# The start of a fused attention and MoE kernel: the decays' polynomial moved from VectorE to GpSimd, weight loads and three conversions moved ahead, half of the decay stores on ScalarE's queue

## The chip, the cores and the metric

The kernel runs on one core of one Trainium2 chip, in one launch. The metric is the device time in microseconds (us), lower is better. A core has TensorE (PE, matmuls), VectorE (DVE), ScalarE (ACT), GpSimd (POOL) and SyncE (SP), which here only issues DMA transfers. Each engine works through its own list of instructions in order and waits at an instruction until what it needs is there.

## The reference

Attention with forget gates on 32 heads (4 x 8) of 576 positions and width 64, then two feed-forward blocks on the 2304 tokens:

```
scores = scale * q @ k.T
log_f  = log(clip(f, 1e-4, 1));  cum = cumsum(log_f)
scores = where(causal, -1e9, scores + cum[i] - cum[j])
x = softmax(scores) @ v                       # heads side by side: 2304 x 512
h = x @ w_in;  x = (h * tanh(softplus(h))) @ w_out
x = (((x @ w1) * (x @ w2)) @ w3) @ w_out2
```

The weights arrive as 64-bit floats (looked at as pairs of 32-bit words), and the kernel turns them into 32-bit numbers itself.

## The kernel before

**Phase A** (to about 350 us) is the attention, 16 pairs of heads, each in four slots (0 to 3): scores into PSUM, softmax, transposes, product with v. Between the pieces of attention PE does filler: first eight units `wp_unit`, which multiply w3 by w_out2, 24 matmuls each, then the first layer's matmuls. **Phase B** is the feed-forward. PE's list is written by hand in both phases. The start, up to the end of the first ten weight pieces, is written by hand for ACT, DVE and SP as well; later work of those engines is placed by a scheduler with priorities and `behind` constraints.

**The start** has two strands. The first is the *decays*: `decay_log` (L249) loads f and computes its logarithm on DVE as exponent plus a polynomial of s, with z = s*s: nine instructions to z, then the polynomial (L264 to L267, nine instructions on 128x144), then e, the exponent's part (L268), and the sum (L269). `decay_rows` (L272) sums it along the positions (L279), adds offsets by a matmul with `heads` (L280, L282), splits it into four rows of high and low parts (`slot`, last written at L288), stores them to DRAM by four SP transfers (L290) and loads them back by `load_cum` (L336) as rows of `aug`. PE's first full scores are the sum of q*k from `raw` and the decays from `aug`, so they wait for the whole strand.

The second strand is the *weight pieces* `first`: t00, o0 to o3, t01, o4 to o7, where t is w3 and o is w_out2, 512 KB each. Each is loaded by SP (`cv_load`, L122), gets its exponents and mantissas by ACT (`cv_exp`, L133) and three DVE instructions (`cv_bits`, L141 to L143), and is then split into a high part by ACT (L98) and a low part by DVE (L102). The first `wp_unit` needs all ten. `go(i)` is the exp and the bits of piece i, `fin(i)` the split. The first softmax is held behind piece number HOLD. The next weight pieces (t10, t11 and on) go the same way, but their low parts are taken by POOL (L112).

POOL's part at the start is `consts` (identity, `heads`, the masks m1 and m4) and in `zeros` (L311) the constant fill of `raw`, `aug`, `pt4` and `vb` for both buffers.

What the change touches stands in this order before (the tenth line converts piece 0 while the matmul of the offsets runs):

```python
        self.consts()
        with self.tc.manual_schedule(engines=...Activation, DVE, SP):
            self.zeros()
            self.decay_log()
            self.load_raw(0)
            early(0, NEAR)
            self.decay_rows(lambda: go(0), lambda: early(NEAR, NEAR + 1))
            early(NEAR + 1, len(first))
            for i in range(1, len(first)):
                go(i); ...; fin(i - 1)
            fin(9)
```

Of the kernel before, what the change touches and what calls it, by code (L numbers as in the profile page):

```python
# [33 lines left out]
KQ = 2 * S + 64  # L34
LAST = 2 * S - 64
HOLD = 4
# [7 lines left out]
NEAR = 4  # L44
# [31 lines left out]
class Kernel:  # L76
# [172 lines left out]
    def decay_log(self):  # L249
# [5 lines left out]
        nc.sync.dma_start(x, self.f)  # L255
        dve.tensor_scalar(x, x, 1e-4, 1.0, ALU.max, ALU.min)
# [7 lines left out]
        dve.tensor_scalar(q, z, 1.0 / 17, None, ALU.mult)  # L264
        for k in (15, 13, 11, 9, 7, 5, 3):
            dve.scalar_tensor_tensor(q, q, 1.0 / k, z, ALU.add, ALU.mult)
        dve.scalar_tensor_tensor(q, q, 1.0, s, ALU.add, ALU.mult)  # L267
        dve.tensor_scalar(e, e, 126.0, 0.6931471805599453, ALU.subtract, ALU.mult)  # L268
        dve.scalar_tensor_tensor(q, q, 2.0, e, ALU.mult, ALU.add)  # L269
        self.lf = q  # L270

    def decay_rows(self, between, after):  # L272
# [6 lines left out]
        dve.tensor_tensor_scan(cum, self.lf, self.lf, 0.0, ALU.add, ALU.bypass)  # L279
# [9 lines left out]
        for i in range(4):  # L289
            nc.sync.dma_start(self.cum_scr[:, :, 144 * i:144 * i + 144], f32(slot[32 * i:32 * i + 32]))  # L290
# [4 lines left out]
    def consts(self):  # L295
# [3 lines left out]
        for i in range(1, 4):  # L299
            nc.gpsimd.affine_select(self.heads, self.heads, [[-1, 128]], ALU.not_equal, 1.0, base=32 * i,  # L300
                                    channel_multiplier=1)
        nc.gpsimd.memset(self.m1, 0.0)
# [8 lines left out]
    def zeros(self):  # L311

        nc = self.nc
        for i in range(2):
            nc.vector.memset(f32(self.aug[i]), 0.0)
            for r in (0, 64):
                nc.gpsimd.memset(f32(self.aug[i][r:r + 4, 0:S]), 1.0)
                nc.gpsimd.memset(f32(self.aug[i][r:r + 4, S:LAST if r else 2 * S]), 1.0)
            nc.gpsimd.memset(f32(self.aug[i][64:68, 2 * S:KQ]), 1.0)
            nc.gpsimd.memset(self.raw[i][0:64, 2 * S:2 * S + 64], 0.0)  # L320
            nc.gpsimd.memset(self.raw[i][64:128, LAST:2 * S], 0.0)
            nc.gpsimd.memset(self.pt4[i][64:128], 0.0)
            nc.gpsimd.memset(self.vb[i][64:128], 0.0)
# [277 lines left out]
    def phase_a(self):  # L601
# [23 lines left out]
        self.consts()  # L625
        self.lo_eng = "dve"
        with self.tc.manual_schedule(engines={getattr(mybir.EngineType, e) for e in ("Activation", "DVE", "SP")}):
# [708 lines left out]
```

## Time and profile before

| | us |
|---|---|
| median of 3 runs | 924.03 (923.31 to 926.38) |
| the profiled execution, its own time | 920.79 |
| its span, first to last instruction | 919.0 |
| PE busy | 873.7 (95%) |
| DVE busy | 688.1 (75%) |
| ACT busy | 483.3 (53%) |
| POOL busy | 166.2 (18%) |

The busy shares are averages over the whole span. The rows further down show the first 60 us, where the change is made. Times in them are from the start of the span; a row that begins with two numbers gives the start and the time of an instruction or of a merged run of equal ones ("x4").

### The profile page before, as it was taken

The numbers are of one execution on the slowest core, as the hardware profiler recorded it, in microseconds if no ns is written. First come the engines' busy times: TensorE is split into PE (matmuls) and PEld (weight loads), VectorE is DVE, ScalarE is ACT, GpSimd is POOL, SyncE is SP. The second block draws the span as 40 slices with busy tenths as digits, with TensorE's granted clock in tenths as the row PEclk, the third lists the DMA queues.
The fourth block names the chain that finished last, engine by engine and source line by source line (L and its number), as shares of the span: only waits on it lengthen the run. The fifth ranks groups of instructions, "written<-read, shape, count | busy, mean of one in ns | idle before, by whom it ended". The sixth has DMA issues, their size and how long they took to land.

```text
span 919.0 us, 17491 instructions
## 1 busy us (share of the span) xinstructions
PE 873.7 (95%) x6338; PEld 806.1 (88%) x6338; DVE 688.1 (75%) x1361; ACT 483.3 (53%) x1035; POOL 166.2 (18%) x253
## 2 busy tenths in 40 slices
PE   2799999999999989799999999999999999999998
PEld 1577778888888758799999999999999999999998
DVE  8987796744767676788888889888788887544483
ACT  3766667655556454655645455455784545322152
POOL 4043333325778740000000000000000000000000
PEclk9899999999999999999999999999999999999999
DMA  6965567757788872244475549988986555555552
GB/s 186 273 193 171 174 195 223 214 159 231 247 274 277 286 239 89 70 138 138 138 229 161 184 165 337 368 316 296 413 303 190 153 168 169 161 164 166 174 166 78
DMA packets 129191, 190.12 MB, mean 207 GB/s; under 512 B 12352, under 2 KB 70736, under 8 KB 129104
## 3 DMA queue, kind: packets, MB, share of 16 engines
q1 hardware_dynamic: 114608, 172.66, 58.2%
q10 hardware_dynamic: 14496, 16.33, 5.8%
q8 instruction: 50, 0.82, 0.4%
q14 instruction: 37, 0.30, 0.1%
HBM read 131.44 MB, written 57.52 MB: 206 GB/s over the span
## 4 chain that ended last, share of the span: by engine, by line
PE 63%; DMA 7%; DVE 7%; POOL 5%; issue 2%; ACT 1%; SPq 0%; ACTq 0%; DVEq 0%; POOLq 0%
PE ps_x L993 15%; PE ps_x L1065 14%; PE ps_z L1065 7%; PE ps_l L552 6%; PE ps_z L993 6%; PE ps_y L993 6%; PE ps_y L1065 3%; DMA ws<-ws 2%; PE ps_s L371 2%; PE ps_s L472 2%; POOL pt L849 2%; DMA ws<-pt 1%; PE ps_t L438 1%; POOL pt L848 1%; DVE TX L955 1%
## 5 line engine op out<-in xcount | busy, mean ns | idle before, releaser
L552 PE MATMUL ps_l<-x,wi 128*128 128x288 f32 x696 | 103.2, 302 | 0.6 <-ACT h L556 0.6
L552 PEld LDWEIGHTS ps_l<-x,wi 128*128 128x128 f32 x696 | 94.8, 190 | 5.7 <-issue 2.8
L954 ACT CAST g_h<-y 128x576 fp32r<-128x576 f32 x96 | 63.6, 675 | 55.0 <-PE ps_x L993 26.1
L993 PE MATMUL ps_x<-g_h,ws 128*128 128x288 f32 x512 | 91.5, 297 | 0.9 <-ACT g_h L954 0.7
L955 DVE TENSOR_TENSOR g_l<-y,g_h 128x576 fp32r<-128x576 f32 x96 | 72.3, 753 | 16.1 <-ACT g_h L954 15.3
L401 ACT ACTIVATE P<-P,sum 128x256 f32<-128x256 f32 (+3 forms) x112 | 70.5, 631 | 24.7 <-DVE sum L391 14.6
L993 PEld LDWEIGHTS ps_x<-g_h,ws 128*128 128x128 f32 x512 | 75.8, 189 | 1.8 <-ACT g_h L954 1.2
L391 DVE CUSTOM_DVE_ANT_0 P<-ps_s,m 128x256 f32<-128x256 f32 (+2 forms) x96 | 48.4, 553 | 18.9 <-PE ps_s L371 18.9
L993 PE MATMUL ps_x<-g_l,ws 128*128 128x288 f32 x256 | 55.2, 297 | 0.5 <-DVE g_l L955 0.5
L453 DVE COPY pt<-ps_t 128x128 f32<-128x128 f32 (+1 forms) x64 | 29.7, 485 | 34.5 <-PE ps_t L438 33.8
L1065 PE MATMUL ps_x<-T,gs 128*128 128x288 f32 x384 | 53.8, 295 | 0.9 <-ACT Cg L1070 0.9
L371 PE MATMUL ps_s<-raw 64*128 64x128 f32 (+3 forms) x256 | 46.6, 476 | 8.3 <-DMA raw<-in_qk_dram 5.9
L1065 PE MATMUL ps_x<-T,ws 128*128 128x288 f32 x384 | 53.8, 295 | 0.0
L1065 PEld LDWEIGHTS ps_x<-T,gs 128*128 128x128 f32 x384 | 51.8, 188 | 1.1 <-ACT Cg L1070 1.1
L1065 PEld LDWEIGHTS ps_x<-T,ws 128*128 128x128 f32 x384 | 51.9, 188 | 0.0
L521 PE MATMUL ps_l<-wo,w3h 128*128 128x512 f32 x128 | 45.3, 423 | 5.2 <-DVE wo L102 4.0
L954 ACT CAST h_h<-ab 128x576 fp32r<-128x576 f32 x48 | 31.7, 673 | 34.0 <-PE ps_x L993 19.9
L993 PE MATMUL ps_x<-h_h,ws 128*128 128x288 f32 x256 | 46.3, 297 | 1.5 <-DMA ws<-ws 1.4
L955 DVE TENSOR_TENSOR h_l<-ab,h_h 128x576 fp32r<-128x576 f32 x48 | 35.9, 754 | 15.6 <-ACT h_h L954 15.5
L472 PE MATMUL ps_s<-pt,va 128*64 128x320 f32 (+3 forms) x384 | 45.0, 383 | 0.0
L438 PE MATMUL ps_t<-ident,P 128*128 128x128 f32 x288 | 40.2, 275 | 2.5 <-ACT pt L453 2.2
L993 PEld LDWEIGHTS ps_x<-g_l,ws 128*128 128x128 f32 x256 | 41.2, 189 | 1.0 <-DVE g_l L955 1.0
(278 smaller groups left out, 2180.0 us busy)
## 6 DMA issues: line engine op xcount, KB each, us to landing
ws<-ws SPq DMA_DIRECT2D x112, 512.0 KB
ws<-gs SPq DMA_DIRECT2D x84, 256.0 KB
ws<-pt SPq DMA_DIRECT2D x45, 256.0 KB
h_scr<-h ACTq DMA_DIRECT2D x64, 144.0 KB
y<-h_scr SPq DMA_DIRECT2D x16, 576.0 KB
cvrt<-in_w3t_dram SPq DMA_DIRECT2D x16, 512.0 KB
cvri<-in_w_in_dram SPq DMA_DIRECT2D x16, 512.0 KB
cvru<-in_w_out_dram SPq DMA_DIRECT2D x16, 512.0 KB
```

The lines of the kernel that those rows point to most:

```text
L371: mm(ps[:, 512 * hh:512 * hh + n], t[r, q0:q0 + 128], t[r, 0:n], start=first, stop=not first)
L391: dve = ttr(P[hh][:, :n], ps[:, 512 * hh:512 * hh + n], self.m1[:, 512 - n:], -0.125, 3.0e38, ALU.add, ALU.min, st[hh])
L401: ins = nc.scalar.activation(t[:, :n], t[:, :n], AF.Exp, bias=b, scale=-1.0, accum_out=self.sums[:, i:i + 1])
L438: tr(self.ps_t[hh][:, o + 128 * k:o + 128 * k + 128], P[:, 128 * k:128 * k + 128], self.ident)
L453: return copy(dst[:, 0:c + 1, 128 * c:128 * c + 128], src)
L472: mm(ps[64 * hh:64 * hh + 64, 256 + q:256 + q + w], lhs, rhs, start=i == 0, stop=i == len(plan) - 1)
L521: mm(o, w, x, start=i == 0, stop=i == 23)
L552: mm(o[:, :TB], w, x, start=i == 0, stop=i == 11)
L954: self.mark(self.nc.scalar.copy(hi, raw))
L955: self.mark(self.nc.vector.tensor_tensor(lo, raw, f32(hi), ALU.subtract))
L993: mm(ps[:, r, :TB], w[:, 256 * a + 128 * e:256 * a + 128 * e + 128], ops[i][b][:, r], start=o in (1, 5, 2) and f == 0 and (a, b) == (0, 0) ...
L1065: mm(bank[:, r, :TB], w[:, i:i + 128], T[o, k][:, b, r], start=o in (1, 2, 5) and (k, a, b) == (0, 0, 0), stop=(k, a, b) == (1, 1, 0), ski ...
```

## The change

The polynomial leaves DVE and becomes sixteen POOL instructions, eight with one input and eight with two, each of which reads the result of the one before. DVE keeps e and the sum, which moves to the head of `decay_rows`. SP loads t00 and o0 ahead of `raw`, and o1, o2, o3 and t01 behind it, before the decay stores (six pieces in place of four). Three pieces (t00, o0, o1) are converted, and two of them split, before `decay_rows`, and o1's split stands where t00's conversion stood. Two of the four decay stores are issued by ACT. POOL's fills are put in order by hand: what the first pair needs, the polynomial, then masks and the second buffers. HOLD is 6, and the slots whose loads stand behind the start's are 0 to 7 (before: 0 and 1).

```diff
-HOLD = 4
+HOLD = 6
...
-NEAR = 4
+NEAR = 6
...
-    def decay_log(self):
+    def decay_log(self, after):
...
         nc.sync.dma_start(x, self.f)
+        after()
...
         dve.tensor_tensor(z, s, s, ALU.mult)
-        dve.tensor_scalar(q, z, 1.0 / 17, None, ALU.mult)
-        for k in (15, 13, 11, 9, 7, 5, 3):
-            dve.scalar_tensor_tensor(q, q, 1.0 / k, z, ALU.add, ALU.mult)
-        dve.scalar_tensor_tensor(q, q, 1.0, s, ALU.add, ALU.mult)
         dve.tensor_scalar(e, e, 126.0, 0.6931471805599453, ALU.subtract, ALU.mult)
-        dve.scalar_tensor_tensor(q, q, 2.0, e, ALU.mult, ALU.add)
-        self.lf = q
+        pool = nc.gpsimd
+        pool.tensor_scalar(q, z, 1.0 / 17, 1.0 / 15, ALU.mult, ALU.add)
+        for k in (13, 11, 9, 7, 5, 3, 1):
+            pool.tensor_tensor(q, q, z, ALU.mult)
+            pool.tensor_scalar(q, q, 1.0 / k, None, ALU.add)
+        pool.tensor_tensor(q, q, s, ALU.mult)
+        self.lf = q, e
...
-        dve.tensor_tensor_scan(cum, self.lf, self.lf, 0.0, ALU.add, ALU.bypass)
+        lf, e = self.lf
+        dve.scalar_tensor_tensor(lf, lf, 2.0, e, ALU.mult, ALU.add)
+        dve.tensor_tensor_scan(cum, lf, lf, 0.0, ALU.add, ALU.bypass)
...
-            nc.sync.dma_start(self.cum_scr[:, :, 144 * i:144 * i + 144], f32(slot[32 * i:32 * i + 32]))
+            (nc.sync, nc.scalar)[i % 2].dma_start(self.cum_scr[:, :, 144 * i:144 * i + 144], f32(slot[32 * i:32 * i + 32]))
...
-        def go(i):
-            self.cv_exp(first[i][0])
-            self.last = self.cv_bits(first[i][0])
...
+        def exp(i):
+            if i < len(first):
+                self.cv_exp(first[i][0])
+
+        def bits(i):
+            exp(i + 1)
+            last = self.cv_bits(first[i][0])
+            if i == HOLD:
+                self.hold = last
...
+            self.consts()
             self.zeros()
-            self.decay_log()
+            self.blanks(0)
+            self.ones(0)
+            self.decay_log(lambda: early(0, 2))
             self.load_raw(0)
-            early(0, NEAR)
-            self.decay_rows(lambda: go(0), lambda: early(NEAR, NEAR + 1))
+            early(2, NEAR)
+            self.masks()
+            self.blanks(1)
+            self.ones(1)
+            exp(0)
+            for i in range(3):
+                bits(i)
+                if i:
+                    fin(i - 1)
+            self.decay_rows(lambda: fin(2), lambda: early(NEAR, NEAR + 1))
             early(NEAR + 1, len(first))
-            for i in range(1, len(first)):
-                go(i)
-                if i == HOLD:
-                    self.hold = self.last
-                fin(i - 1)
+            for i in range(3, len(first)):
+                bits(i)
+                if i > 3:
+                    fin(i - 1)
             fin(9)
...
-                with self.behind(self.go_sp if s < 2 else None):
+                with self.behind(self.go_sp if s < 8 else None):
```

PE's list has the same 2155 rows in the same order. The lists of the other engines differ at the start, as shown next, and here and there by one place near the end of phase B.

DVE's list at the decays, before: `lg` holds the logarithm's temporaries, `cvt` and `cvo` are pieces, `cu` the decays' rows.

```order
L263 TENSOR_TENSOR lg_152<-lg_151 128x144
L264 TENSOR_SCALAR lg_152<-lg_152 128x144
L266 SCALAR_TENSOR_TENSOR lg_152<-lg_152 128x144 x7
L267 SCALAR_TENSOR_TENSOR lg_152<-lg_152,lg_151 128x144
L268 TENSOR_SCALAR lg_151<-lg_151 128x144
L269 SCALAR_TENSOR_TENSOR lg_152<-lg_152,lg_151 128x144
L279 SCALAR_TENSOR_TENSOR cu_185<-lg_152 128x144
L141 TENSOR_SCALAR cvt_189<-cvt_189 128x512
L142 SCALAR_TENSOR_TENSOR cvt_189<-cvrt_177,cvt_189 128x512
L143 SCALAR_TENSOR_TENSOR cvt_189<-cvrt_177,cvt_189 128x512
L282 COPY cu_185<-ps_l_82 128x1
```

The same place of the change, from the last piece that is converted ahead of the decays (the conversions of t00 and o0 and t00's low part stand just before these rows, behind z and e):

```order
L141 TENSOR_SCALAR cvo_202<-cvo_202 128x512
L142 SCALAR_TENSOR_TENSOR cvo_202<-cvro_167,cvo_202 128x512
L143 SCALAR_TENSOR_TENSOR cvo_202<-cvro_167,cvo_202 128x512
L102 TENSOR_TENSOR wo_0_216<-cvo_197,wo_0_216 128x512
L282 SCALAR_TENSOR_TENSOR lg_132<-lg_132,lg_131 128x144
L283 SCALAR_TENSOR_TENSOR cu_219<-lg_132 128x144
L102 TENSOR_TENSOR wo_1_224<-cvo_202,wo_1_224 128x512
L286 COPY cu_219<-ps_l_82 128x1
```

The nine polynomial rows are gone, the scan (L279, now L283) stands behind three conversions, and only one low part stands between it and the copy of the offsets.

POOL's list of the change, from the last fill of the first pair's `aug` on; the eleven alternating rows left out are of the same two kinds:

```order
L328 MEMSET aug_95 4x512
L329 MEMSET aug_95 4x64
L267 TENSOR_SCALAR lg_132<-lg_132 128x144
L269 TENSOR_TENSOR lg_132<-lg_132 128x144
L270 TENSOR_SCALAR lg_132<-lg_132 128x144
...
L271 TENSOR_TENSOR lg_132<-lg_132,lg_131 128x144
L309 MEMSET m_86 128x512
L310 MEMSET m_87 128x288
L311 AFFINE_SELECT m_86<-m_86 128x128
```

Before, these sixteen rows did not exist and POOL had no arithmetic until the low part of t10.

DVE's list a little later, where t10 and t11 are converted, the pieces that PE needs for its second `wp_unit` (before, t10 is cvt_337 and t11 cvt_384; `P` rows are softmax):

```order
L141 TENSOR_SCALAR cvt_337<-cvt_337 128x512
L397 ISA P_0_103,sum_307<-ps_s_79,m_86 128x288
L397 ISA sum_307 128x1
L142 SCALAR_TENSOR_TENSOR cvt_337<-cvrt_321,cvt_337 128x512
L398 ISA P_0_103,sum_307<-ps_s_79,m_87,sum_307 128x288
L398 ISA sum_307 128x1
L141 TENSOR_SCALAR cvt_384<-cvt_384 128x512
L143 SCALAR_TENSOR_TENSOR cvt_337<-cvrt_321,cvt_337 128x512
```

And with the change (t10 is cvt_344, t11 cvt_391):

```order
L411 ISA P_0_103,sum_314<-ps_s_79,m_86 128x288
L411 ISA sum_314 128x1
L102 TENSOR_TENSOR wo_7_300<-cvo_286,wo_7_300 128x512
L412 ISA P_0_103,sum_314<-ps_s_79,m_87,sum_314 128x288
L412 ISA sum_314 128x1
L141 TENSOR_SCALAR cvt_344<-cvt_344 128x512
L141 TENSOR_SCALAR cvt_391<-cvt_391 128x512
L142 SCALAR_TENSOR_TENSOR cvt_344<-cvrt_328,cvt_344 128x512
L142 SCALAR_TENSOR_TENSOR cvt_391<-cvrt_330,cvt_391 128x512
L143 SCALAR_TENSOR_TENSOR cvt_344<-cvrt_328,cvt_344 128x512
```

t10 is finished one row later in relation to what surrounds it: t11's second instruction (L142) now stands ahead of t10's last.

## Rows read from the trace of the kernel before

**Rows 1.** PE's waits in the first 48 us: total, times, longest.

```profile
PE ps_s L371 <- DMA aug<-cum_scr: 9.5, 1, 9.5
...
PE ps_l L521 <- DVE wo L102: 4.0, 2, 2.3
```

**Rows 2.** Windows: stretch, busy us of PE to POOL, granted clock, DMA share, GB/s.

```profile
34.00:36.00 2.00, 0.70 (x2) 0.60 (x3) 2.00 (x6) 1.41 (x5) 0.00 (x0) 0.67 1.09 240
...
40.00:42.00 2.00, 2.00 (x8) 1.59 (x6) 1.76 (x6) 1.67 (x4) 0.00 (x0) 0.62 0.97 247
...
50.00:60.00 10.00, 10.00 (x54) 7.32 (x52) 8.36 (x26) 7.99 (x25) 1.44 (x2) 1.00 0.46 149
```

**Rows 3.** PE's timeline: first full scores, last transposes before t10, t10's first matmuls.

```profile
20.75 1.38 PE L371 MATMUL ps_s<-aug 64*128 64x128 f32 x4 [9.46 <-DMA aug<-cum_scr]
...
42.10 0.84 PE L438 MATMUL ps_t<-ident,P 128*128 128x128 f32 x6
44.11 0.74 PE L521 MATMUL ps_l<-wo,w3h 128*128 128x512 f32 x2 [1.17 <-ACT w3h L98]
```

**Rows 4.** DVE's timeline, the decays from behind z to the last slot row.

```profile
6.13 0.23 DVE L264 TENSOR_SCALAR lg<-lg 128x144 f32<-128x144 f32 x1
...
9.07 0.67 DVE L268 TENSOR_SCALAR lg<-lg 128x144 f32<-128x144 f32 x1
9.78 0.31 DVE L269 SCALAR_TENSOR_TENSOR lg<-lg,lg 128x144 f32<-128x144 f32 x1
10.12 0.46 DVE L279 TENSOR_TENSOR_SCAN cu<-lg 128x144 f32<-128x144 f32 x1
...
12.40 0.15 DVE L282 COPY cu<-ps_l 128x1 f32<-128x1 f32 x1
...
13.53 0.23 DVE L288 TENSOR_SCALAR cu<-cu 128x144 fp32r<-128x144 f32 x1
```

**Rows 5.** PE's timeline: the matmul of the offsets.

```profile
10.73 0.56 PE L280 MATMUL ps_l<-cu,heads 128*128 128x1 f32 x2 [2.44 <-DVE cu L279]
```

**Rows 6.** SP's timeline: the four decay stores.

```profile
13.85 2.58 SPq L290 DMA_DIRECT2D cum_scr<-cu x4
```

**Rows 7.** DVE's timeline: start of one piece's bits, the low part behind, the next bits.

```profile
16.49 0.42 DVE L141 TENSOR_SCALAR cvo<-cvo 128x512 int32<-128x512 int32 x1
...
18.27 0.68 DVE L102 TENSOR_TENSOR wo<-cvo,wo 128x512 fp32r<-128x512 f32 x1
18.87 0.42 DVE L141 TENSOR_SCALAR cvo<-cvo 128x512 int32<-128x512 int32 x1
```

**Rows 8.** DVE's timeline: an idle, t10's last instruction, one of t11 beside POOL.

```profile
14.09 0.43 DVE L141 TENSOR_SCALAR cvo<-cvo 128x512 int32<-128x512 int32 x1 [0.33 <-ACT cvo L133]
...
42.43 0.68 DVE L143 SCALAR_TENSOR_TENSOR cvt<-cvrt,cvt 128x512 int32<-128x512 int32 x1
...
44.56 1.11 DVE L143 SCALAR_TENSOR_TENSOR cvt<-cvrt,cvt 128x512 int32<-128x512 int32 x1
```

**Rows 9.** POOL's timeline: a fill, arithmetic beside busy and idle DVE, a dependent pair.

```profile
5.19 0.57 POOL L317 MEMSET aug<- 4x576 f32 x1
...
44.21 4.35 POOL L112 TENSOR_TENSOR w3l<-cvt,w3h 128x256 fp32r<-128x256 f32 x4 [33.09 <-ACT w3h L98]
54.26 1.44 POOL L112 TENSOR_TENSOR w3l<-cvt,w3h 128x256 fp32r<-128x256 f32 x2 [5.70 <-ACT w3h L98]
...
68.35 1.57 POOL L112 TENSOR_TENSOR x<-xx,x 128x288 fp32r<-128x288 f32 x2 [2.32 <-ACT x L98]
...
302.90 0.40 POOL L848 CAST pt<-cvu 128x256 fp32r<-128x256 f32 x1
...
304.12 0.85 POOL L848 CAST pt<-cvu 128x256 fp32r<-128x256 f32 x1
...
306.77 0.72 POOL L829 TENSOR_TENSOR pt<-cvu,cvu 128x256 f32<-128x256 f32 x1
307.57 0.73 POOL L830 TENSOR_TENSOR pt<-pt,cvu 128x256 f32<-128x256 f32 x1
```

More of the change, by code (lines that the diff above doesn't have):

```diff
@@ L301, in consts, with masks @@
                                     channel_multiplier=1)
+    def masks(self):
+        nc = self.nc
         nc.gpsimd.memset(self.m1, 0.0)
@@ L311, in zeros, with ones, blanks @@
     def zeros(self):
+        for i in range(2):
+            self.nc.vector.memset(f32(self.aug[i]), 0.0)
+    def ones(self, i):
         nc = self.nc
[L314 to L323, printed above, removed]
+        for r in (0, 64):
+            nc.gpsimd.memset(f32(self.aug[i][r:r + 4, 0:S]), 1.0)
+            nc.gpsimd.memset(f32(self.aug[i][r:r + 4, S:LAST if r else 2 * S]), 1.0)
+        nc.gpsimd.memset(f32(self.aug[i][64:68, 2 * S:KQ]), 1.0)
+    def blanks(self, i):
+        nc = self.nc
+        nc.gpsimd.memset(self.raw[i][0:64, 2 * S:2 * S + 64], 0.0)
+        nc.gpsimd.memset(self.raw[i][64:128, LAST:2 * S], 0.0)
+        nc.gpsimd.memset(self.pt4[i][64:128], 0.0)
+        nc.gpsimd.memset(self.vb[i][64:128], 0.0)
     def load_raw(self, p):
@@ L616, in early @@
                 self.cv_load(first[i][0], first[i][1], where[i])
-        def go(i):
-            self.cv_exp(first[i][0])
-            self.last = self.cv_bits(first[i][0])
         def fin(i):
             first[i][2](*first[i][3:])
-        self.consts()
+        def exp(i):
[6 more added lines that the diff above has]
+                self.hold = last
         self.lo_eng = "dve"
-        with self.tc.manual_schedule(engines={getattr(mybir.EngineType, e) for e in ("Activation", "DVE", "SP")}):
+        engines = {getattr(mybir.EngineType, e) for e in ("Activation", "DVE", "SP", "Pool")}
+        with self.tc.manual_schedule(engines=engines):
+            self.consts()
             self.zeros()
-            self.decay_log()
+            self.blanks(0)
+            self.ones(0)
+            self.decay_log(lambda: early(0, 2))
             self.load_raw(0)
-            early(0, NEAR)
-            self.decay_rows(lambda: go(0), lambda: early(NEAR, NEAR + 1))
-            early(NEAR + 1, len(first))
-            for i in range(1, len(first)):
-                go(i)
-                if i == HOLD:
-                    self.hold = self.last
-                fin(i - 1)
+            early(2, NEAR)
[8 more added lines that the diff above has]
+            self.decay_rows(lambda: fin(2), lambda: early(NEAR, NEAR + 1))
+            early(NEAR + 1, len(first))
+            for i in range(3, len(first)):
+                bits(i)
+                if i > 3:
+                    fin(i - 1)
             fin(9)
```

## The prediction

> **What bounds the kernel now.** First the waits of PE in the first 48 us, since the change touches nothing else: the largest is 9.5 us for the decays' rows, then 4.0 us in two pieces for low parts of o pieces [rows 1]. Next the windows: from 50 us PE is busy without a gap (10.00 of 10.00) [rows 2], so what counts is the moment from which PE no longer waits. PE's timeline gives it: its last transposes of the start end at 42.94, it waits 1.17 us for ACT's high part of t10, and starts t10's matmuls at 44.11 [rows 3]. I call this moment T. Whatever moves T moves the end of the kernel by as much, if the clock stays what it was.
>
> What sets T is DVE, not the decays. In the windows DVE is busy 2.00 of 2.00 us at 34 to 36 and 1.76 at 40 to 42 [rows 2]; t10's high part waits for t10's last DVE instruction, which ends at 43.11 [rows 8], and of DVE's idle ahead of it only 0.33 us is worth a row [rows 8]. So the 9.5 us wait of PE is no loss by itself: PE catches up and waits for DVE again. A change is worth what it takes off DVE's list ahead of t10, less what it adds there as work or waiting.
>
> **The change part by part.** I use one mark, S, the end of the last slot row: 13.53 + 0.23 = 13.76 before [rows 4]. From S to T it is 44.11 - 13.76 = 30.35 us.
>
> *Removed from DVE.* The polynomial runs from 6.13 to 9.07, 2.94 us [rows 4].
>
> *Ahead of S, added.* Three pieces' bits and two low parts. Bits take 18.27 - 16.49 = 1.78, a low part 18.87 - 18.27 = 0.60 [rows 7], together 3 x 1.78 + 2 x 0.60 = 6.54. DVE has z at 6.13; e's step (9.07 to 9.78 before, beside POOL's fills) I take at 0.4, so the conversions run from 6.5 to 13.05 if nothing slows them. Their loads now leave SP first; o0 and o1 have 1.8 and 4.2 us of DVE work ahead of them as cover, and t00 alone could be late, at most by the tenths that POOL's polynomial hides anyway.
>
> *The polynomial on POOL.* Fifteen fills go ahead of it: five of `aug` at no more than 0.57 [rows 9] and ten shorter ones, so POOL is free at about 6 and the start is set by z, 6.1. Before has no POOL arithmetic on 144 columns. From 256 and 288 columns (1.44 / 2 = 0.72, 1.57 / 2 = 0.785) a two-input instruction costs 2.0 ns a column and 0.21 fixed, so 0.50 on 144; with the same fixed part the one-input cast (0.40 on 256) costs 0.75 ns a column, so 0.32. An instruction that reads the one before starts 307.57 - 306.77 - 0.72 = 0.08 late [rows 9]. Eight pairs of 0.50 + 0.32 + 2 x 0.08 = 0.98 are 7.8 us: undisturbed, the polynomial ends at 13.9.
>
> It isn't undisturbed. Where POOL's two-input instructions meet DVE's conversions, POOL's take 4.35 / 4 = 1.09 for 0.72 [rows 9], and DVE's 1.11 for 0.68 [rows 8]. POOL loses 0.37 and DVE 0.43 for each 256 x 2.0 ns = 0.51 that POOL streams, 0.73 and 0.84 of it. The polynomial streams 8 x 144 x (2.0 + 0.75) ns = 3.2 us. POOL loses 2.3 and ends at 16.2; DVE loses 2.7 and ends its conversions at 15.75, before POOL. The bounds are 13.9 (no loss), and, with each two-input one at 1.09 / 0.72 and each one-input one at 0.85 / 0.40 [rows 9], 8 x (0.76 + 0.68 + 0.16) = 12.8, an end at 18.9. I take 16.2, since DVE will be as busy there as at 44 us.
>
> *To S.* Sum 0.34 (9.78 to 10.12), scan to the end of the matmul 11.29 - 10.12 = 1.17 [rows 4, 5], 0.1 for the hand-over, copy to the last slot row 13.76 - 12.40 = 1.36 [rows 4]; o1's low part (0.60) lies inside the matmul's time. S = 16.2 + 2.97 = 19.2, **5.4 us later** than before.
>
> *From S to T.* Gone from the 30.35 are the bits of o0 and o1 and the low parts of t00, o0 and o1, 2 x 1.78 + 3 x 0.60 = 5.36, and the idle of 0.33 ahead of o0 [rows 8]. New are t11's L142 ahead of t10's last instruction, one step of about 0.60, and a wait for o3's exponents: ACT issues its two stores first, 2 x 0.645 = 1.29 [rows 6], against 1.78 of o2's bits as cover; with the exponents' own time behind it I put the wait at 0.25. That leaves 25.5, and T = 19.2 + 25.5 = **44.7, 0.6 later** than before.
>
> *The stores and the other edits.* Two queues issue 1.29 us each in place of 2.58 on one [rows 6]. Full scores then start at S + 0.09 + 1.29 and the 20.75 - 16.43 = 4.32 from the last issue to PE: 24.9, where before it was 20.75. Worth nothing at T while PE can catch up: its work from 20.75 to 42.94 is 22.2 us with 4.0 of idle, so it could be done at 24.9 + 18.2 = 43.1, 1.6 ahead of T. HOLD puts the first softmax on DVE behind four pieces' bits and two low parts, at S + 8.3; its scores end 5.7 + 1.38 [rows 3] behind S, so it doesn't wait. SP's list holds o4 and the later loads behind the stores, some 5 us later than before; DVE needs them some 5 us later too. POOL's masks and second fills move behind the polynomial, to about 16 to 22; the first softmax wants m1 at S + 8.3, near 27.5. Slots 2 to 7 behind the start's loads cost nothing as long as SP's list stays in its old order, which it nearly does.
>
> **The sum.** T moves by +0.6, the profiled execution from 920.79 to 921.4; on the median of the runs, which is 3.2 above that execution, 924.03 becomes **924.6**. No change beyond 0.3% (2.8 us), about what a measurement can tell from no change; the three runs of before lie 3.1 apart.
>
> **The rivals.**
> *POOL runs undisturbed* (chance 0.15). Its short instructions might fall between DVE's, and a fixed part of 0.21 in each leaves room for that. Then the end is 13.9, S 16.9, T 42.4: **-1.7, 922.3**. Against it: both engines lose in rows 8 and 9. The limit is DVE's own end at 13.05: S 16.0, T 41.5, -2.6, and no polynomial, however fast, gives more.
> The Trainium skill, GPSIMD Engine Reference, section 4.1, puts two-input work on GpSimd at about twice VectorE's time and one-input work near its rate. With VectorE's 0.31 and 0.23 that estimate is 8 x (0.62 + 0.23) = 6.8 us, an end at 12.9 and the -2.6. The same page, section 8, says that GpSimd shares its SBUF interfaces with VectorE and contends with two-input instructions and with two-port modes. The trace agrees with section 8, 1.09 for 0.72, and that speaks against using 4.1's ratio beside a busy VectorE.
>
> *POOL is starved* (0.10). One-input instructions at 0.85, as the cast beside a conversion: end 18.9, S 21.9, T 47.4, **+3.3, 927.3**. Against: DVE runs out of conversions at about 16, and POOL is alone from there.
>
> *The clock falls just ahead of T* (0.20), the case on the other side by one mechanism. Before, PE was granted half speed (1.2 of 2.4 GHz) from about 34.7 to 41.5 (0.67 over 34 to 36, 0.62 over 40 to 42 [rows 2]), after the two idles that make 4.0 us [rows 1]. It cost nothing there, since PE waited again at 42.94. Now those idles vanish, because pieces are ready when PE starts late, and PE is faster and idles in front of T instead: 1.6 us, or up to 5.0 if the half-speed stretch, worth 6.8 / 2 = 3.4, is gone. If the grant falls there, the half speed lies where PE has no slack: half as long as before costs 1.7, as long 3.4; T's +0.6 with it gives **+2.3 to +4.0, 926.3 to 928.0**. It decides as soon as half speed reaches 2.2 / 0.5 = 4.4 us beyond T. Against: the 1.17 us idle at 42.94 brought no fall.
>
> *PE's chain becomes the bound*: only if T came before 43.1 with S as late as 19.2; included in the forecast's width.
>
> **How the numbers follow.** The forecast has 0.50 (T between -0.9 and +2.1), the rivals 0.15, 0.10 and 0.20, and 0.05 is left for what I don't see, mostly shifts in phase B's scheduler order. The range reaches to the undisturbed limit, 924.03 - 2.6 = 921.4, and to the long clock case, 928.0. Faster by over 0.3% takes the limit of the first rival plus scatter: 0.12. Slower takes half of the clock rival, most of the starved one and some scatter of the forecast: 0.26. Within 0.3%: 0.62.
>
> **What would show it.** POOL's sixteen instructions from about 6.1 to 16.2, one-input ones over 0.32; DVE's L142 and L143 near 1 us in that time, 0.69 after; S near 19.2; full scores near 24.9; PE's first matmul of t10 near 44.7, with an idle ahead of it; a granted clock of 1.00 there. I am wrong if the polynomial ends before 14, if DVE isn't what PE waits for at t10, or if the time differs and T doesn't.

## The result, and the profile of the changed kernel

The change takes 929.17 us (median of 9 runs, 927.43 to 933.47) where the kernel before, run beside it, takes 921.51 (9 runs, 917.32 to 926.38): ratio 1.0077, 95% interval 1.0052 to 1.0101, **7.7 us slower**. On another chip it was 1.0065 (1.0040 to 1.0089). The profiled execution took 929.95 us, its span is 928.0. The prediction counts from 924.03, the median of three of the nine runs of before, so it is read here by differences and ratios.

PE's waits in the first 60 us: total, times, longest. Left out are two that end ahead of the full scores: for `raw`, 8.2 us, and of the offsets' matmul, 9.5 us.

```profile
...
PE ps_s L385 <- DMA aug<-cum_scr: 7.8, 1, 7.8
PE ps_l L535 <- ACT w3h L98: 2.8, 1, 2.8
PE ps_l L535 <- DVE wo L102: 1.9, 1, 1.9
...
```

PE's timeline: start, us, instruction, and the idle ahead of it with what ended it.

```profile
28.48 1.29 PE L385 MATMUL ps_s<-aug 64*128 64x128 f32 x4 [7.81 <-DMA aug<-cum_scr]
...
42.96 0.51 PE L535 MATMUL ps_l<-wo,w3h 128*128 128x512 f32 x1 [1.91 <-DVE wo L102]
...
48.13 0.73 PE L535 MATMUL ps_l<-wo,w3h 128*128 128x512 f32 x2 [2.81 <-ACT w3h L98]
```

The full scores start at 28.48 (20.75 in [rows 3]), and T, the first matmul of t10, is 48.13 (44.11 in [rows 3]): 4.0 us later. The o pieces' waits shrink from 4.0 to 1.9 us, and the wait right ahead of T grows from 1.17 to 2.81.

DVE's timeline, from the decays' first step to the first piece behind them; first the steps to e, then the first and the last instruction of the conversions ahead, the sum, the last slot row, and o3.

```profile
3.33 0.49 DVE L257 TENSOR_SCALAR lg<-lg 128x144 f32<-128x144 f32 x1
...
6.89 0.23 DVE L265 TENSOR_SCALAR lg<-lg 128x144 f32<-128x144 f32 x1
7.03 0.42 DVE L141 TENSOR_SCALAR cvt<-cvt 128x512 int32<-128x512 int32 x1
...
14.31 0.78 DVE L102 TENSOR_TENSOR wo<-cvo,wo 128x512 fp32r<-128x512 f32 x1
19.16 0.31 DVE L282 SCALAR_TENSOR_TENSOR lg<-lg,lg 128x144 f32<-128x144 f32 x1 [4.06 <-POOL lg L271]
...
21.84 0.67 DVE L292 TENSOR_SCALAR cu<-cu 128x144 fp32r<-128x144 f32 x1
...
24.89 0.43 DVE L141 TENSOR_SCALAR cvo<-cvo 128x512 int32<-128x512 int32 x1 [0.65 <-ACT cvo L133]
```

POOL's timeline: the polynomial, in three pieces of it.

```profile
7.15 0.47 POOL L267 TENSOR_SCALAR lg<-lg 128x144 f32<-128x144 f32 x1 [1.40 <-DVE lg L265]
7.70 0.82 POOL L269 TENSOR_TENSOR lg<-lg 128x144 f32<-128x144 f32 x1
8.61 1.06 POOL L270 TENSOR_SCALAR lg<-lg 128x144 f32<-128x144 f32 x1
...
16.19 0.49 POOL L269 TENSOR_TENSOR lg<-lg 128x144 f32<-128x144 f32 x1
16.76 0.57 POOL L270 TENSOR_SCALAR lg<-lg 128x144 f32<-128x144 f32 x1
...
18.64 0.49 POOL L271 TENSOR_TENSOR lg<-lg,lg 128x144 f32<-128x144 f32 x1
```

DVE has its conversions done at 14.31 + 0.78 = 15.1 and then waits 4.06 us for POOL, whose polynomial runs from 7.15 to 19.13, 11.98 us. S, the end of the last slot row, is 21.84 + 0.67 = 22.51 (13.76 before, 19.2 predicted). From S to T it is 25.6 us, where the prediction had 25.5.

Windows behind T: stretch, busy us of PE, PEld, DVE, ACT and POOL with their counts, granted clock, DMA share, GB/s.

```profile
48.00:50.00 2.00, 1.22 (x3) 0.79 (x4) 1.97 (x4) 1.18 (x3) 1.77 (x2) 0.72 0.47 105
50.00:52.00 2.00, 2.00 (x6) 1.52 (x6) 0.00 (x1) 0.00 (x0) 2.00 (x3) 0.50 0.92 253
...
54.00:56.00 2.00, 2.00 (x13) 1.68 (x13) 0.12 (x1) 0.69 (x2) 0.00 (x0) 0.57 0.71 240
56.00:58.00 2.00, 2.00 (x17) 1.65 (x16) 1.75 (x10) 1.29 (x6) 0.00 (x0) 1.00 0.00 1
```

PE is granted half speed (1.2 of 2.4 GHz) from about 49 to 55.7, behind its 2.8 us of idle, and in the windows from 50 on it is busy without a gap. One more mark closes the start: L, PE's first matmul of the first layer, here of before, then of the change.

```profile
131.91 3.44 PE L552 MATMUL ps_l<-x,wi 128*128 128x288 f32 x24
```
```profile
138.70 3.44 PE L566 MATMUL ps_l<-x,wi 128*128 128x288 f32 x24
```

L is 6.8 us late in this execution (5.2 in a second one, further down), which is most of the loss. From L to the end of the span it is 787.1 us before and 789.3 with the change, and between 784.6 and 795.5 in the 18 profiled executions of this study without an order by kernel; that part is the scatter of an execution. So S, T and L are what the experiments are read by, all in us. They come from one profiled execution each, the ratios from the medians of several runs:

| run | S | T | L | ratio to before (95%) |
|---|---|---|---|---|
| before | 13.76 | 44.11 | 131.9 | 1 |
| the change | 22.51 | 48.13 | 138.7 | 1.0077 (1.0052 to 1.0101) |
| the change, again | 22.69 | 48.62 | 137.1 | 1.0065 (1.0040 to 1.0089) |
| polynomial on DVE | 19.69 | 45.49 | 134.0 | 1.0046 (1.0019 to 1.0074) |
| two-operation form | 21.06 | 47.15 | 136.1 | 1.0033 (1.0003 to 1.0062) |
| five pieces ahead | 25.39 | 51.81 | 140.2 | 1.0087 (1.0057 to 1.0116) |
| before, polynomial on POOL | 24.25 | 55.17 | 144.0 | 1.0138 (1.0096 to 1.0180) |
| before, DVE polynomial twice | 16.51 | 47.62 | 135.3 | 1.0004 (0.9978 to 1.0031) |
| before, three times | 19.53 | 49.89 | 137.7 | 1.0049 (1.0025 to 1.0073) |
| the change, PE kept busy | 22.87 | 48.34 | 137.6 | 1.0057 (1.0026 to 1.0088) |
| the same, again | 22.21 | 47.63 | 137.0 | 1.0082 (1.0050 to 1.0114) |
| Ln on ScalarE, words first | 12.63 | 44.21 | 133.3 | 0.9986 (0.9960 to 1.0013) |
| the same, PE kept busy | 11.45 | 42.33 | 129.8 | 0.9994 (0.9964 to 1.0025) |
| Ln, early rows | 9.35 | 42.42 | 131.5 | 1.0000 (0.9975 to 1.0025) |

### The profile page after: what moved, and what is told of

Same layout as the page of the kernel before. It is cut to its first block, busy times and chain, and to the rows that moved or that the text cites. A ratio compares the mean times of both kernels' runs of the same rounds, so it can differ in the third digit from the quotient of the medians.

```text
span 928.0 us, 17507 instructions
## 1 busy us (share of the span) xinstructions
PE 874.1 (94%) x6338; PEld 807.8 (87%) x6338; DVE 683.6 (74%) x1352; ACT 483.4 (52%) x1035; POOL 176.4 (19%) x269
## 4 chain that ended last, share of the span: by engine, by line
PE 54%; DVE 5%; DMA 5%; ACT 1%; issue 1%; SPq 0%; DVEq 0%; ACTq 0%
PE ps_x L1095 15%; PE ps_x L1023 14%; PE ps_z L1095 8%; PE ps_z L1023 6%; PE ps_y L1023 6%; PE ps_y L1095 4%; DMA ws<-ws 3%; DVE TX L985 1%; PE ps_l L566 1%; DMA R<-inv_scr 1%; PE ps_s L385 1%; DMA w_scr<-cvv 0%; DVE g_l L985 0%; DMA cvru<-in_w_out_dram 0%; DMA ws<-pt 0%
## 5 line engine op out<-in xcount | busy, mean ns | idle before, releaser
L415 ACT ACTIVATE P<-P,sum 128x256 f32<-128x256 f32 (+3 forms) x112 | 70.5, 631 | 25.5 <-DVE sum L405 12.7
## 6 DMA issues: line engine op xcount, KB each, us to landing
h_scr<-h ACTq DMA_DIRECT2D x64, 144.0 KB
```

The source lines that it names most:

```text
L415: ins = nc.scalar.activation(t[:, :n], t[:, :n], AF.Exp, bias=b, scale=-1.0, accum_out=self.sums[:, i:i + 1])
```

## The experiments

### Which part of the change costs: the polynomial back on DVE

```diff
-        pool.tensor_scalar(q, z, 1.0 / 17, 1.0 / 15, ALU.mult, ALU.add)
...
+        dve.tensor_scalar(q, z, 1.0 / 17, None, ALU.mult)
+        for k in (15, 13, 11, 9, 7, 5, 3):
+            dve.scalar_tensor_tensor(q, q, 1.0 / k, z, ALU.add, ALU.mult)
+        dve.scalar_tensor_tensor(q, q, 1.0, s, ALU.add, ALU.mult)
```

> The change with the polynomial alone put back on VectorE, right behind z; loads, order of the pieces, stores and HOLD stay as changed. My theory: the change is slower because the polynomial takes 12 us on GpSimd (S at 22.5), and because PE then idles ahead of t10's first matmul (T, at 48.1) and falls to half speed just behind it. Then here z ends near 7, the polynomial near 9.8, three pieces take 6.5 without contention, S is near 19.5 and T near 45 (25.6 behind S, as in the change): 3 us less than the change if the half speed still follows T, 6 to 7 less if not; 922 to 926. Rival, the loads and pieces put first (raw lands later, ACT waits for loads) are what costs: then T stays near 48 and the time near 929.

925.69 us (12 runs), within what was expected. PE's timeline of this run:

```profile
45.49 1.22 PE L533 MATMUL ps_l<-wo,w3h 128*128 128x512 f32 x2 [2.56 <-ACT w3h L98]
```

T returns to 45.49 and S to 19.69. Of the 4.0 us at T the polynomial's place is worth 2.6; the order of loads and conversions alone still costs 1.4: S is 5.9 later than before, and the way from S to T only 4.55 shorter. S is near the predicted 19.2 here, and the ratio is still 1.0046 and not 1.0006. Its interval overlaps the change's, so what the medians gain by this edit isn't clear of noise; T and L show it.

### What the polynomial costs on GpSimd alone: no pieces ahead

The three conversions ahead of `decay_rows` stand behind it, all else as in the change.

```diff
-            for i in range(3):
-                bits(i)
-                if i:
-                    fin(i - 1)
-            self.decay_rows(lambda: fin(2), lambda: early(NEAR, NEAR + 1))
+            self.decay_rows(lambda: None, lambda: early(NEAR, NEAR + 1))
...
-            for i in range(3, len(first)):
+            for i in range(len(first)):
...
```

> The change with no piece converted ahead of the decays, so that GpSimd has the polynomial to itself; all pieces follow behind the slot rows. It measures the undisturbed price of the sixteen instructions. With the rows of the change where VectorE sat idle (0.57 for one input, 0.49 for two, 0.08 between) they take 8 x 1.22 = 9.8 us; by my prediction's prices 7.8. Contention in the change is then 12.0 less this. VectorE idles all that time, so T comes later than in the change, near 51, and the time is 2 to 3 us longer.

One run, 938.03 us. POOL's timeline, with DVE idle for 9.5 us:

```profile
7.15 0.31 POOL L267 TENSOR_SCALAR lg<-lg 128x144 f32<-128x144 f32 x1 [1.40 <-DVE lg L265]
7.55 0.49 POOL L269 TENSOR_TENSOR lg<-lg 128x144 f32<-128x144 f32 x1
8.12 0.58 POOL L270 TENSOR_SCALAR lg<-lg 128x144 f32<-128x144 f32 x1
...
16.14 0.49 POOL L271 TENSOR_TENSOR lg<-lg,lg 128x144 f32<-128x144 f32 x1
```

Undisturbed, the polynomial takes 16.63 - 7.15 = 9.48 us. The two-input price (0.49) and the dependent gap (7.55 - 7.15 - 0.31 = 0.09) are as predicted (0.50, 0.08); the one-input price isn't, 0.57 against 0.32. Contention in the change is then 11.98 - 9.48 = 2.5 us (predicted 2.3). T came at 52.25, a little later than expected, and L at 140.8, 2.1 us behind the change's; both fit the conversions that DVE didn't do in those 9.5 us and that follow behind. The time was a miss, 9 us over the change's for the expected 2 to 3, and most of that lies behind L (795.5 us to the end for 789.3), where this single run shows no cause.

### Whether that price belongs to the form of the instruction

```diff
-            pool.tensor_scalar(q, q, 1.0 / k, None, ALU.add)
+            pool.tensor_scalar(q, q, 1.0, 1.0 / k, ALU.mult, ALU.add)
```

> The change with its seven one-input steps on GpSimd written with two operations (times 1.0, plus 1/k) where they had one (plus 1/k). Theory (the price belongs to the form): in the changed kernel's trace the one-operation form took 0.57 us and the two-operation form 0.47 beside VectorE, and where GpSimd had the time to itself 0.57 against 0.31; so seven times 0.26 = 1.8 us come out of the polynomial (12.0 to 10.2 us), the last slot row ends 1.8 us earlier (22.5 to 20.7), the first product of t10 starts near 46.3, and the time is 1 to 2 us under the change's if the half-speed stretch stays. Rival (the price belongs to the instruction's place in the chain, not to its form): 0.57 stays, and T stays at 48.1.

Median 925.66 us (10 runs). POOL's timeline, one such step beside DVE and the last one without it:

```profile
8.61 0.63 POOL L270 TENSOR_SCALAR lg<-lg 128x144 f32<-128x144 f32 x1
...
16.80 0.31 POOL L270 TENSOR_SCALAR lg<-lg 128x144 f32<-128x144 f32 x1
17.20 0.49 POOL L271 TENSOR_TENSOR lg<-lg,lg 128x144 f32<-128x144 f32 x1
```

The price belongs to the form: with a multiplication by one that changes nothing, 0.57 becomes 0.31, and beside DVE 1.06 becomes 0.63. The polynomial ends at 17.69, 1.4 us earlier (expected 1.8), S is 1.45 earlier, T 1.0. Against the expected 1 to 2 us the medians lie further apart (1.0033 against 1.0077), but the intervals overlap.

### The polynomial's move without the rest of the change

Only the sixteen POOL instructions, put into the kernel before.

```diff
-        dve.tensor_scalar(q, z, 1.0 / 17, None, ALU.mult)
...
+        pool.tensor_scalar(q, z, 1.0 / 17, 1.0 / 15, ALU.mult, ALU.add)
...
```

> The kernel before with the polynomial alone moved to GpSimd; order of loads, fills and stores as before. Theory (the polynomial's time on GpSimd is the loss): VectorE's 2.9 us of polynomial become 9.5 us or more, behind GpSimd's own fills; nothing that is converted meanwhile pays for it, so T (44.1 before) comes 6.5 us later or more, near 51, and a half-speed stretch behind T, if there is one, adds up to 3.4 us: 928 to 932. Rival (the other parts of the change lose the time): T stays under 47 and the time under 926.

935.23 us (4 runs). First DVE's sum, then PE's first matmul of t10:

```profile
20.40 0.31 DVE L271 SCALAR_TENSOR_TENSOR lg<-lg,lg 128x144 f32<-128x144 f32 x1 [14.06 <-POOL lg L269]
```
```profile
55.17 0.73 PE L523 MATMUL ps_l<-wo,w3h 128*128 128x512 f32 x2 [3.19 <-ACT w3h L98]
```

The move alone costs 13 us (1.0138; 8.9 to 16.6), more than I expected: POOL starts at 10.90, behind its own fills, and DVE stands for 14 us. The change as a whole, at 6 to 8 us, costs about half of that.

### More cover for the polynomial: five pieces ahead

```diff
-            for i in range(3):
+            for i in range(5):
                 bits(i)
...
-            self.decay_rows(lambda: fin(2), lambda: early(NEAR, NEAR + 1))
+            self.decay_rows(lambda: fin(4), lambda: early(NEAR, NEAR + 1))
```

> The change with five pieces (t00, o0 to o3) converted ahead of the decays in place of three, so that VectorE has work while it waits 4.1 us for the polynomial. My theory: VectorE's wait goes, the polynomial ends 0.5 to 1.5 later by contention, S is at 23 to 24, S to T is 25.6 less two bits and two low parts (4.8), T near 44.3 or wherever PE's own list lets it (full scores at S + 5.7, some 15 us of work behind them). PE has little idle ahead of T, so the clock holds: 6 to 7 us less than the change, 922 to 923, about as before. Rival, S sets the time, since PE starts its full scores 7.7 us later than before: then this run is no faster than the change, or slower by the 0.5 to 1.5 us.

931.12 us (9 runs), a miss: no faster than the change, as the rival had it. DVE's longest waits and PE's first matmul of t10:

```profile
DVE cvo L141 <- ACT cvo L133: 4.2, 1, 4.2
...
DVE w3l L102 <- ACT w3h L98: 2.7, 2, 1.6
```
```profile
51.81 1.21 PE L535 MATMUL ps_l<-wo,w3h 128*128 128x512 f32 x2 [3.60 <-ACT w3h L98]
```

DVE's 4 us of waiting are filled, but the conversions then end at 22.1, past the polynomial (19.7), and the idle only moves: the next piece waits 4.2 us for its exponents, whose words stand behind the decay stores on SP's queue.

### The stores on one queue

```diff
-            (nc.sync, nc.scalar)[i % 2].dma_start(...)
+            nc.sync.dma_start(...)
```

> The change with the four stores of the decay rows all on SP's queue, as before. Theory (the split of the stores has no part in the loss): the full scores of pair 0 start 1 to 1.5 us later than the change's 28.5, T at 48.1 moves by less than 0.5 us either way. Rival (ScalarE's queue or the wait for its stores delays the conversions): T comes 1 us or more earlier.

One run, 927.33 us. The full scores come at 29.84 (28.48), as expected, but T at 49.88, 1.75 later than the change's, which neither theory had: 0.4 is S (22.90), the rest comes behind the stores, where the loads of the later pieces wait on the same queue (three of them are issued at 28.75, in the change at 27.51). So there is no sign that the split loses time. That it helps isn't shown: it is one run, and its time is not above the change's.

### Lateness alone: the DVE polynomial two and three times

```diff
+        for _ in range(3):
+            dve.tensor_scalar(q, z, 1.0 / 17, None, ALU.mult)
+            for k in (15, 13, 11, 9, 7, 5, 3):
...
```

> The kernel before with the decays' polynomial computed twice on VectorE (the second time over the first), nothing else changed: pure lateness of 2.9 us for the decay rows. Theory (the loss is the lateness of t10's first product, T, plus the clock at half speed behind it): T comes near 47.0 (44.1 before), and the time is 2.9 to 6.3 us over before's, the upper end if the trace shows half speed behind T. Rival (the change loses by something else that it does: fills, stores, GpSimd): lateness is taken up by other slack, and the time is under 1.5 us over before's.

> The kernel before with the decays' polynomial computed three times on VectorE, nothing else changed: lateness of 5.9 us. Theory: T near 50.0, the time 5.9 to 9.3 us over before's, the upper end if the trace shows half speed behind T; the change's +4.0 of T and +7.7 of time should lie between this run and the one with the polynomial twice, or close to them. Rival: under 3 us over before's.

924.99 us for twice, 927.27 for three times (12 runs each, before 923.67 beside them). T and L follow S: with three times S is 5.8 late, T 5.8, L 5.8, and the ratio is 1.0049 (2.3 to 6.7 us). PE's first matmul of t10 there, and the windows ahead of it:

```profile
49.89 0.73 PE L522 MATMUL ps_l<-wo,w3h 128*128 128x512 f32 x2 [1.09 <-ACT w3h L98]
```
```profile
42.00:44.00 2.00, 2.00 (x9) 1.71 (x8) 1.97 (x5) 1.52 (x5) 0.00 (x0) 0.50 0.27 71
```

So with three times the lateness of the decays, with nothing else of the change, costs about what it delays. The half-speed stretch (40 to 47) lies ahead of T here, as in before [rows 2], and PE still waits 1.09 us behind it, so it doesn't set T. With the polynomial twice it is otherwise: T and L are 3.5 and 3.4 late, but by the ratio the median is only 0.4 us over before's (-2.0 to +2.9). That is what the rival of that run said (under 1.5 us), and the 3.4 of L lies outside the interval.

### The clock: TensorE kept busy ahead of T

Twelve matmuls whose result is overwritten, in the idle ahead of t10's first product, in the change (twice) and five of them in the kernel before; the last pair of runs has the unaltered change beside it on one chip.

```diff
+            if i == 0 and f == FS[1]:
+                for _ in range(12):
+                    mm(o, self.w3s[FS[0]][0][:, 0:128], self.wo2t[0][:, 0:512], start=True, stop=True)
             mm(o, w, x, start=i == 0, stop=i == 23)
```

> The change with twelve more matmuls on PE just ahead of t10's first one, into the bank that it overwrites (their results are used nowhere). They fill about 2.6 us of the 2.8 us idle. My theory: T stays at 48.1 to 48.4, the granted clock stays at full speed behind it, the 6.8 us of half speed at 48.9 to 55.7 vanish, and 3.4 us come back: 925.8. Rival, the half speed costs nothing since PE waits for other engines in that stretch anyway: the same time as the change, 929.

> The kernel before with five extra matmuls, whose result is overwritten, ahead of t10's first product, nothing else. Theory (the clock's fall ahead of T is a cost of its own, which the wait there brings): in the profiled execution of before the clock was whole behind T, so the extra matmuls change its fast executions by nothing or cost up to 1 us (TensorE waits there for 2 us anyway), and at most they remove some of the slow end of the spread: 921 to 923, the lowest time as before. Rival (the extra matmuls themselves make the kernel faster or slower, so that the run of the change with twelve of them tells nothing of the clock): the lowest and the median move by 2 us or more.

> The change itself, beside the next run on the same chip, with a profile of another execution. Theory: T near 48.1, a wait of 2.5 us or more ahead of it, half speed behind it for 6 to 7 us; 6 to 8 us over before. Rival (the half speed of the first profile was that execution's alone): whole speed behind T, and the time is 4 us over before's.

> The change with twelve extra matmuls, whose result is overwritten, ahead of t10's first product, beside the change on the same chip. Theory (half speed behind T is part of the loss): 2 to 3.4 us under the change's median, whole speed behind T in the trace. Rival (the lateness of T is the whole loss, the clock none): the same median within 1 us.

With the extra matmuls the change took 927.62 us (1.0057, 1.0026 to 1.0088), between theory and rival, and, beside the change itself, 928.87 (1.0082, 1.0050 to 1.0114) against 929.07 (1.0065): the same, as the rival said. Before with five of them took 925.65 (1.0024, 0.9999 to 1.0049). Its lowest time and median are about 3 us over those of before, which is what the rival of that run named: the extra matmuls may cost something themselves. Its trace shows 0.2 us of that at L (132.15). Behind T, first the change again, then with the extra matmuls, and PE's timeline of the latter from t10's first product on:

```profile
50.00:52.00 2.00, 2.00 (x5) 1.52 (x5) 0.19 (x1) 0.46 (x1) 2.00 (x3) 0.50 0.92 203
52.00:54.00 2.00, 2.00 (x14) 1.73 (x12) 0.00 (x0) 0.46 (x1) 0.19 (x1) 0.97 1.06 378
```
```profile
50.00:52.00 2.00, 2.00 (x16) 1.57 (x14) 0.23 (x1) 0.00 (x0) 1.53 (x2) 1.00 0.98 327
```
```profile
47.63 0.68 PE L538 MATMUL ps_l<-wo,w3h 128*128 128x512 f32 x2
...
56.95 0.66 PE L456 MATMUL ps_t<-ident,P 128*128 128x128 f32 x4 [1.34 <-ACT pt L467]
```

The second execution of the change has half speed behind T again, but for about 3.4 us instead of 6.8. With the extra matmuls the clock is whole, PE runs ahead, and then stands 1.34 us for a softmax row from ACT at 56.95, a wait that the change itself doesn't have; in the first run with them it is 1.43. L is 137.1 without and 137.0 with them. From T to L it is 87.8 us before, 90.6 and 88.5 in the two executions of the change, and 89.3 in both with the clock whole: the way behind T is some 1.5 us longer than before even at whole speed, about the softmax wait. The Trainium skill, TensorE: Matmul & The Clock Gate, section Why this matters for your kernels, advises against idle of PE between bursts, since the clock drops to half. The clock of these rows agrees with it (0.50 behind an idle of 2.8 and 3.1 us, 1.00 with the idle filled); the time doesn't follow here, because the saved time is waited away.

The granted clock isn't the whole of it. PE's timeline of the change, two equal matmuls in windows whose row says 1.00:

```profile
30.72 0.63 PE L535 MATMUL ps_l<-wo,w3l 128*128 128x512 f32 x1
...
37.16 0.40 PE L535 MATMUL ps_l<-wo,w3l 128*128 128x512 f32 x1
```

Where the row says 0.50 such a matmul takes 0.63 (at 50.96). So PE seems to run at half speed behind the idle ahead of the full scores too (7.8 us here), in before (0.63 at 23.08) as in the runs with extra matmuls, and the rows of the granted clock don't tell it; no run tests this.

### The other direction: earlier decays

The logarithm becomes one ScalarE instruction, in place of the exponent, mantissa and polynomial steps on DVE. First with t00 and o0 loaded ahead of `raw`, without and with twelve extra matmuls as above; then with the loads of before, GpSimd building `heads` and filling `raw` ahead of `aug`, the masks last, and t00 converted behind the slot rows, without and with five extra matmuls.

```diff
-        dve.tensor_scalar(u.bitcast(I32), x.bitcast(I32), 23, None, ALU.logical_shift_right)
...
-        dve.scalar_tensor_tensor(q, q, 2.0, e, ALU.mult, ALU.add)
+        nc.scalar.activation(q, x, AF.Ln)
```

> The kernel before with the words loaded first, and the decays' logarithm as one ScalarE instruction (Ln) in place of VectorE's exponent, mantissa and polynomial steps, which are left out. Theory (everything behind the decays moves with the end of the last slot row): the steps from the words to the scan, 9.8 us of the time before, become one instruction of about 0.5 us and perhaps a function table's load of 1 to 2 us on ScalarE; the last slot row ends 4 to 5 us earlier (13.8 to about 9), and T moves from 44.1 to 39 or 40: 4 to 5 us faster, 917 to 919 against a before of 922, less up to 3.4 us if the clock falls to half behind T. Rival (T is then set by the conversions of the first pieces and by their loads, not by the decays): T moves by 2 us or less and the time stays within 2 us of before.

> The run before this one (logarithm on ScalarE, words first) with twelve extra matmuls, whose result is overwritten, ahead of t10's first product, so that TensorE doesn't stand idle there. Theory (a half-speed stretch behind T takes part of the gain): without a fall of the granted clock the time is 1 to 3.4 us under that of the run without the extra matmuls, if that one's trace shows a half-speed stretch near T. Rival (no half-speed stretch there): the extra matmuls cost nothing or up to 1 us.

> The kernel before with the decays' logarithm as one ScalarE instruction (Ln) in place of VectorE's exponent, mantissa and polynomial steps, which are left out; words loaded as before; GpSimd builds the matrix heads ahead of its fills; the first piece is converted behind the slot rows, not between. Theory (T hangs on the end of the last slot row, once nothing else holds the offsets' matmul): in the run with the logarithm and the words first that matmul waited for the q and k rows' loads and then for heads, until 10.6; here it runs at 6 or so, the last slot row ends near 8.5, and T comes at 36 to 39 (44.1 before): 917 to 919 against a before of 922 to 923, with half speed behind T taking part of it. Rival (the pieces' words and VectorE's and ScalarE's conversions hold T): T stays at 41 or later, and the time within 2 us of before.

> The run before this one with five extra matmuls, whose result is overwritten, ahead of t10's first product. Theory (half speed behind T takes part of the gain): if the trace of the run without them shows half speed behind T, this one is 1 to 3 us faster; if it shows whole speed, the same within 1 us.

None is measurably faster than before: 920.84 (0.9986), 920.78 (0.9994, 0.9964 to 1.0025), 923.33 (1.0000) and 922.09 (1.0000, 0.9976 to 1.0024). In the first the offsets' matmul waits for the rows of `raw`, which the words now precede; in the third that is gone. DVE's timeline of the third, the last slot row and t00's first instruction, and then PE's first matmul of t10:

```profile
8.96 0.39 DVE L276 TENSOR_SCALAR cu<-cu 128x144 fp32r<-128x144 f32 x1
9.95 0.43 DVE L141 TENSOR_SCALAR cvt<-cvt 128x512 int32<-128x512 int32 x1 [0.60 <-ACT cvt L133]
```
```profile
42.42 0.73 PE L513 MATMUL ps_l<-wo,w3h 128*128 128x512 f32 x2 [3.13 <-ACT w3h L98]
```

S is 4.4 us earlier than before and T only 1.7. Conversions can't start before their words and exponents are there, and t00's bits, which before filled DVE's wait for the offsets' matmul, now follow it. In front of T a wait of 3.1 us appears, with half speed behind it. Without the decays' work in DVE's list the start is bound by the pieces, and the rival held in both. The extra matmuls brought no measurable time. Five did not fill PE's idle (a wait of 1.84 us and half speed behind T); with twelve the clock is whole behind T and L is 129.8 in place of 133.3 (in that execution S is 1.2 earlier, too), yet the medians are 920.78 and 920.84.

## Why the prediction was wrong

**The forecast itself, within 0.3%, fell**: T moved by +4.0 and not +0.6, and the time by 0.8%, beyond the upper end of the range. The step that failed first is *the polynomial on POOL*, put at 6.1 to 16.2 and measured at 7.15 to 19.13, with one term of *To S* behind it.

- *The price of a one-input instruction*, 0.32 by way of POOL's cast, is 0.57 in the form that the change uses: 7 x 0.25 = 1.75 us, and the whole polynomial takes 9.48 undisturbed where the sum had 7.8, 1.7 more. Only the first step, with its two operations, has the predicted price (0.31). The bound at 18.9 covered the end (19.13) nearly, by a mechanism that is only half of it: one-input steps take 0.62 to 1.06 beside DVE, and 0.57 from 15 us on where DVE is idle.
- *The start*. I took z as ready at 6.1 as in before. POOL's fills of `aug` now run beside the decays' first steps, and three of DVE's short instructions take 0.49 to 0.66 where they took 0.17 to 0.23 in the run with POOL's move alone. z ends 0.87 later and POOL starts 0.18 behind it: the polynomial starts at 7.15, 1.05 later. The prediction had the row that warned of it (0.67 for e beside fills [rows 4]) and used it only for e.
- *Behind the polynomial* the last slot row stands beside POOL's second fills, 0.67 for 0.23: +0.4.

With 0.2 of contention these are 1.7 + 1.05 + 0.4 + 0.2 = 3.35, against the 3.3 by which S missed.

The case that came nearest is the *starved* rival (0.10): its end, S and T are 18.9, 21.9 and 47.4, the measured ones 19.13, 22.51 and 48.13. What spoke against it, that POOL is alone from about 16, was no help, since the one-input form takes 0.57 alone as well.

The other step that failed is *whatever moves T moves the end by as much*: T moved by 4.0 and 4.5 in the two executions of the change, L by 6.8 and 5.2.

**Right**: the two-input price, the dependent gap, the size of the contention on POOL's side (2.5 for 2.3), that DVE runs out of conversions before POOL (by 0.45 in the sum, 4.06 measured), and that PE waits at T for a piece and not for the decays. The way from S to T (25.6 for 25.5) is in part luck: the wait for o3's exponents was 0.65 for 0.25, and ACT's list added 0.3 behind t10's last DVE instruction (46.11 + 0.68 = 46.79, T at 48.13; before 43.11 and 44.11), which shorter places elsewhere took back. DVE's own loss by contention was about 1 us, not 2.7; this cost the sum nothing, since POOL ended later. The full scores came 6.0 behind S, as in the sum (5.7).

**The clock rival** was kept as a case of its own on top of +0.6. Half speed did come behind T, in both profiled executions of the change, so its step was right as a place. Its price is not shown: stretches worth 1.7 and 3.4 us came with L at +5.2 and +6.8, but with the clock whole L was still at +5.05 and +5.7, and the time the same. Behind T the change's two executions lose 0.7 and 2.8 us against before, and the two with the clock whole 1.5, by a softmax wait; how much of the median is clock, these runs can't tell. The range ended at 928.0 because I let lateness and clock exclude each other; the starved case with this clock would have been +5.0 to +6.7.

**Not settled**: the polynomial twice on DVE delays L by 3.4 us and the median by 0.4 (at most 2.9), while the polynomial on DVE within the change delays L by 2.1 and the median by 4.2 (1.8 to 6.8). In the two kernels with Ln and the words first L differs by 3.5 and the median by nothing. The way from L to the end shows no order by kernel, so I take these as the scatter of medians of about a dozen runs, whose intervals are over 4 us wide; no run tells it for sure. So the lateness of T is shown in the traces, and that lateness costs time by the runs with the move alone (+13) and with three polynomials (+4.5); how the change's 6 to 8 us divide between T and what comes behind it stays open. HOLD and the slots behind the start's loads were not run by themselves; with the loads and conversions they share the 1.4 us of T and the 1.0046 that stay with the polynomial on DVE.

By the Trainium skill, GPSIMD Engine Reference, section 4.1, two-input work on GpSimd takes about twice VectorE's time and one-input work is near its rate; by this estimate the polynomial took 6.8 us. The rows say 9.48 undisturbed. The two-input step is within the rule, 0.49 against VectorE's 0.31; the one-input step with one operation is not, 0.57 against 0.23, and here the measurement decides; with two operations it is 0.31. The rest of the distance to VectorE's 2.94 us is that GpSimd needs sixteen instructions for nine, with a gap of 0.09 at each. Section 8 of that page, on contention, agrees with the 2.5 us.

## What to carry to other kernels

Price an instruction on a slow engine by a row of the very form, operations and all: the price taken from a one-input cast was off by 0.25 us, and a chain multiplies that. A chain of short dependent steps pays the fixed part and the gap at every step, so moving it to another engine is only free if the receiving engine's own time, with contention, ends before the work that was to cover it. Follow one mark near the end of the changed stretch through all runs (here L): it tells where time is lost when medians scatter by several us, though not what the median will be (here twice it moved by 3.4 and 3.5 us and the median did not).

## What the runs showed of the hardware

- On GpSimd a one-operation `tensor_scalar` (add) on 128x144 took 0.57 us and a two-operation one (multiply, add) 0.31, in the same chain and place, without VectorE beside it.
- Beside memsets on GpSimd two of VectorE's short instructions took 0.49 and 0.67 us that took 0.17 and 0.23 in runs without a memset of `aug` beside them (the first step in the run with the move alone, the last slot row in the run with the polynomial on DVE).
- Contention between GpSimd's polynomial and VectorE's conversions cost both: GpSimd 2.5 us on 9.5, and VectorE 8.1 us (7.03 to 15.1, 0.31 of it a wait for ScalarE) for conversions that took 6.9 with the polynomial on DVE (10.00 to 16.86).
- By the rows of the granted clock, half speed stood in the first 60 us of every profiled execution but the two of the change with TensorE kept busy. Where it lay ahead of T alone, L - T was 87.8 before and 87.7 and 87.8 with the polynomial two and three times. Where it reached T or lay behind it, L - T was 88.4 to 90.6; but it was 89.3 in the two with TensorE kept busy as well.
- A 128x512 matmul took 0.63 us in windows with a granted clock of 0.50 and 0.40 in windows with 1.00, but 0.63 also at 30.72 in the change, where the row says 1.00.
